# Key parts without GpSimd, weights prepared a place later: one opening of a four-layer attention kernel

## The chip, the cores and the metric

The kernel runs on one core of a Trainium2 chip. The metric is the device time of one execution in microseconds (us); the time before is the median of three runs. The engines are named as in the profile: PE is TensorE's matrix products (PEld its weight loads), DVE is VectorE, ACT is ScalarE, POOL is GpSimd, SP is SyncE, which only issues transfers here.

## What is computed

Four residual layers, A, B, A, B, over a sequence of 2048 tokens of 640 features in 32 heads of 20; both A layers share their weights, and so do both B layers. The change touches the first layer A only:

```python
phi = lambda t: jnp.where(t > 0, t + 1, jnp.exp(t)) + 1e-6
pq, pk = phi(q), phi(k)
kv = jnp.einsum("bhsd,bhse->bhde", pk, v)
z = jnp.einsum("bhsd->bhd", pk)
num = jnp.einsum("bhqd,bhde->bhqe", pq, kv)
den = jnp.einsum("bhqd,bhd->bhq", pq, z)[..., None] + 1e-6
o = num / den
# x = x + A(layernorm(x)); x = x + B(layernorm(x)); twice
```

Layer B is a block-wise softmax attention with a memory; it is not touched.

## The kernel before

**Tiles and segments.** The sequence is cut into four segments of 512 tokens, each of four tiles of 128. Every float32 operand of a product is held as two float16 parts, a high part (rounded) and a low part (what is left), and a product is three float16 products. A weight is prepared by `w_prep`: load into a staging buffer (two of them), the largest magnitude by five reductions on DVE (L239), a transpose and a broadcast on PE (L247, L253) with small steps on DVE between them (L244, L249), a power-of-two scale, then five casts on ACT for the high parts (L263) and five operations on DVE for the low parts (L264, called its splits here), and a store to DRAM. Seven weights are prepared in the opening: q, v and o of layer A, then v, q, k and o of layer B (Bv, Bq, Bk, Bo); k of layer A comes ahead of all.

**The first layer A** runs in `opening`, which weaves two streams: the main one is `g_first` for a segment, the other (`aux`) gets two steps (three in segment 0) after each of its steps. A step is a piece of a generator up to its `yield`; a step with nothing to do only lets time pass.

- `keys(i)`: for both halves of a tile a projection on PE (L394, fifteen products), exp and relu on ACT (L406, L408) and their combination e on DVE (L409). Here, in the first layer (`L["early"]`): e times a scale on POOL (L531), the high part on ACT (L532), the low part on POOL (L533), and the sum z of all keys (L541; a copy, L539, for the first tile), on DVE in segment 0 and on POOL from then on. In the second layer A the scale is taken along by ACT (L535) and DVE (L536), and POOL has no part in it.
- `queries(i)`: the same projection, then 1e-6 is added (L547, on POOL in the first layer, on DVE in the second) and the half is written to DRAM from SP's queue (L548).
- `memory()`: the products of keys and normalized input, x-hat (`xs`), ten groups of twelve (L562), added up on DVE (L567, L569).
- `merge`, at the end of segment 3: z is summed over tokens by a product with a square of ones (L610 sets it on POOL, L614 is the product), reciprocals on DVE (L616 to L620), then ten pieces `ge` (L634 to L637) and products with the value and output weights (L650, L682, L687), which give one matrix for the layer's second half.

**Beside it** `aux` holds the layer norm of the next segment (`norms`: statistics on DVE, a power on POOL in L342, x-hat on ACT in L367), its transposes on PE (`turn`: L318, high part on ACT in L322, low part on DVE in L323), its two parts (`parts`: L475 on ACT, L476 on POOL), and the weights. In segment 0: the remaining turns of this segment and weight q by turns, then the next segment's norms, then v. Segment 1: norms, o, the constants, Bv. Segment 2: norms, Bq, Bk. Segment 3: Bo, the gates, the head of the second half.

**What sets the order.** PE runs in the order of the program. The other engines' orders are laid out by a planner from priorities and estimated times; `issue_after(ins)` puts what is traced in it behind an instruction on that instruction's engine. Every engine works its own list in order, so an instruction that waits holds up all behind it. Buffers: eight PSUM banks; five buffers (`pq`) for the e of keys and queries; eleven row buffers.

Of the kernel before, what the change touches and what calls it, by code (L numbers as in the profile page):

```python
# [2 lines left out]

# [1 line left out]

# [8 lines left out]
AF = mybir.ActivationFunctionType  # L14
OP = mybir.AluOpType
AX = mybir.AxisListType
# [4 lines left out]
S, D, H, DH = 2048, 640, 32, 20  # L21
P = 128
C = D // P
# [5 lines left out]
HN = 320  # L29
# [113 lines left out]
class Kernel:  # L143
# [81 lines left out]
        return self.sb.tile([P, C, 2, D], F16, tag="wo" if o else "w", name="w_%s%s" % key,  # L225
                            bufs=2 if o else 3)

    def w_prep(self, key, stage, w, wait=0):


        nc, cp = self.nc, self.cp
        st = stage.tile([P, C, D], F32, tag="stage", name="stage", bufs=2)
        src = self.w_src(key).rearrange("(c p) n -> p c n", p=P)
        mx = cp.tile([P, C], F32, name="wmx", tag="wmx", bufs=2)
        for c in range(C):
            nc.sync.dma_start(st[:, c], src[:, c])
        yield from pause(wait)
        for c in range(C):
            nc.vector.tensor_reduce(mx[:, c:c + 1], st[:, c], axis=AX.X, op=OP.max,  # L239
                                    apply_absolute_value=True)  # L240
        yield 0.0
        yield 0.0
        m1 = cp.tile([P, 1], F32, name="wm1", tag="wm1", bufs=2)
        nc.vector.tensor_reduce(m1, mx, axis=AX.X, op=OP.max)  # L244
        yield 0.0
        pt = self.bank()
        nc.tensor.transpose(pt[:1, :P], m1, self.ident)  # L247
        m2 = cp.tile([1, 1], F32, name="wm2", tag="wm2", bufs=2)
        self.last = nc.vector.tensor_reduce(m2, pt[:1, :P], axis=AX.X, op=OP.max)  # L249
        yield 100.0  # L250
        yield from pause(wait)
        pb = self.bank()
        nc.tensor.matmul(pb[:, :1], self.ones, m2, start=True, stop=True)  # L253
        inv = cp.tile([P, 1], F32, name="inv_%s%s" % key)
        scl = cp.tile([P, 1], F32, name="scl_%s%s" % key)
        nc.vector.tensor_scalar(inv.bitcast(I32), pb[:, :1].bitcast(I32), 0x7F800000, None,
                                op0=OP.bitwise_and)
        nc.vector.tensor_scalar(inv, inv, 2.0 ** -14, 2.0 ** -114, op0=OP.mult, op1=OP.max)
        self.last = nc.vector.reciprocal(scl, inv)
        self.inv[key], self.scl[key] = inv, scl  # L260
        yield 100.0
        for c in range(C):
            nc.scalar.activation(w[:, c, 0], st[:, c], AF.Copy, scale=scl)  # L263
            self.last = nc.vector.scalar_tensor_tensor(w[:, c, 1], st[:, c], scl, w[:, c, 0],  # L264
                                                       op0=OP.mult, op1=OP.subtract)
            if c < C - 1:
                yield 0.0
        wd = self.dr.tile([P, C, 2, D], F16, name="wd_%s%s" % key)
        nc.sync.dma_start(wd, w)
        self.wd[key] = wd  # L270
        yield 0.0
# [39 lines left out]
    def turn(self, src, dst, i):  # L311

        nc = self.nc
        for c0, c1 in ((0, 3), (3, 5)):
            pt = self.bank()
            n = c1 - c0
            for c in range(c0, c1):
                nc.tensor.transpose(pt[:, (c - c0) * P:(c - c0 + 1) * P], src[:, c * P:(c + 1) * P],  # L318
                                    self.ident)
            v = pt[:, :n * P].rearrange("p (c t) -> p c t", c=n)  # L320
            hi = dst[:, c0:c1, 0, i * P:(i + 1) * P]
            nc.scalar.activation(hi, v, AF.Copy)  # L322
            nc.vector.tensor_tensor(dst[:, c0:c1, 1, i * P:(i + 1) * P], v, hi, op=OP.subtract)  # L323
            yield n * 110.0

    def load_x(self, src, s, i, name="x"):
# [187 lines left out]
    def g_first(self, s, box, w, L, behind=None):  # L514
# [7 lines left out]
        def keys(i):  # L522
            pk.append(sb.tile([P, 2, D + 1], F16, tag="row", name="pk", bufs=ROWS))
            nc.gpsimd.memset(pk[i][:, 0, HN:HN + 1], 1.0)
            nc.gpsimd.memset(pk[i][:, 1, HN:HN + 1], 0.0)
            for n in range(2):
                z, c = slice(n * HN, (n + 1) * HN), slice(n * (HN + 1), n * (HN + 1) + HN)
                e = self.phi_a(self.proj_n(xT, w("k"), i, n), self.inv["A", "k"])
                hi, lo = pk[i][:, 0, c], pk[i][:, 1, c]
                if L["early"]:  # L530
                    nc.gpsimd.tensor_tensor(e, e, self.k_scl.to_broadcast([P, HN]), op=OP.mult)  # L531
                    nc.scalar.activation(hi, e, AF.Copy)  # L532
                    nc.gpsimd.tensor_tensor(lo, e, hi, op=OP.subtract)  # L533
                else:
                    nc.scalar.activation(hi, e, AF.Copy, scale=self.k_scl)  # L535
                    nc.vector.scalar_tensor_tensor(lo, e, self.k_scl, hi, op0=OP.mult, op1=OP.subtract)  # L536
                vec = nc.gpsimd if L["early"] and s > 0 else nc.vector
                if s == 0 and i == 0:
                    vec.tensor_copy(L["z"][:, z], e)  # L539
                else:  # L540
                    vec.tensor_tensor(L["z"][:, z], L["z"][:, z], e, op=OP.add)  # L541
                yield self.COST_N

        def queries(i):
            for n in range(2):
                e = self.phi_a(self.proj_n(xT, w("q"), i, n), self.inv["A", "q"])
                (nc.gpsimd if L["early"] else nc.vector).tensor_scalar(e, e, 1e-6, None, op0=OP.add)  # L547
                nc.sync.dma_start(L["pqd"][s][i][:, n * HN:(n + 1) * HN], e)  # L548
                yield self.COST_N

        def memory():
# [41 lines left out]
    def merge(self, L, wv, wo, memory, fill):  # L593
# [13 lines left out]
        zb = sb.tile([P, MW], F32, tag="mem", name="zb", bufs=2)  # L607
        rz = self.row("rz")
        square = sb.tile([P, 512], F32, tag="er", name="square", bufs=3)[:, :P]
        nc.gpsimd.memset(square, 1.0)  # L610
        for n in range(2):
            c = slice(n * HN, (n + 1) * HN)
            p = self.bank()[:, :HN]
            nc.tensor.matmul(p, square, L["z"][:, c], start=True, stop=True)  # L614
            if L["early"]:
                nc.vector.tensor_scalar(zb[:, c], p, self.k_inv, S * 1e-6, op0=OP.mult, op1=OP.add)  # L616
            else:
                nc.vector.tensor_scalar(zb[:, c], p, S * 1e-6, None, op0=OP.add)
            nc.vector.reciprocal(rz[:, c], zb[:, c])
            nc.vector.tensor_scalar(rz[:, c], rz[:, c], self.k_inv, G_ONE, op0=OP.mult, op1=OP.mult)  # L620
            yield 4 * HN * COL
# [448 lines left out]
    def opening(self, src, stage, L, box):  # L1070
# [3 lines left out]
        def prep(key, keep=True):  # L1074
            w = self.w_tile(key) if keep else stage.tile([P, C, 2, D], F16, tag="split", name="split", bufs=1)
            if keep:
                self.w[key] = w
            yield from self.w_prep(key, stage, w, 0 if key[0] == "A" and keep else 3)

        def a(n):  # L1080
            if n not in preps:
                preps[n] = prep(("A", n), n in "kq")
            return preps[n]
# [6 lines left out]
        def late():  # L1090
            self.setup_late(stage)
            yield 0.0

        def last():
            self.scales("B")
            self.gates()
            yield 0.0
# [18 lines left out]
        m = [m]  # L1116
        with self.tc.issue_after(self.last.ins):
            m += [self.moments(x[i]) for i in range(2, NT)]
        top = self.taken

        def others():
            self.parts(first, cur[2], 0)
            for i in range(1, NT):
# [1 line left out]
                yield from self.turn(xh, cur[1], i)  # L1125
                self.parts(xh, cur[2], i)

        def later(gen):
            with self.tc.issue_after(top.ins):
                r = next(gen)  # L1130
            yield r
            yield from gen

        o = others()
        self.ones_columns()
        for s in range(NSEG):
            nxt = []
            if s == 0:
                aux = chain(turns(o, later(a("q"))), self.norms(src, 1, nxt, 6), a("v"))
            elif s == 1:  # L1140
                aux = chain(self.norms(src, 2, nxt, 6), a("o"), late(), prep(("B", "v"), False))
            elif s == 2:
                aux = chain(self.norms(src, 3, nxt, 6), prep(("B", "q"), False), prep(("B", "k"), False))
            else:
                self.scales("A")
                self.w["A", "v"] = self.fetch(("A", "v"))
                aux = chain(prep(("B", "o")), last(), self.a_head(L, 0, box))
            use = w if s < NSEG - 1 else lambda n: self.w["A", n]
            yield from weave(self.g_first(s, cur, use, L), aux, per=2 if s else 3)
            cur = nxt  # L1150
# [139 lines left out]
```

## Time and profile before

| | us |
|---|---|
| median of 3 runs (lowest, highest) | 1757.29 (1756.29, 1758.80) |
| the profiled execution | 1756.07 |
| its span, first to last instruction | 1754.4 |
| PE busy in the span | 1659.4 |
| DVE / ACT / POOL busy | 1231.1 / 991.2 / 604.6 |
| mean granted clock of PE | 0.99 |

In the profile a group's row has line, engine, operation, output and inputs, count, then busy time and mean duration in ns, then the idle time of the engine just before these instructions and what ended most of it. A timeline row has start and length in us and, in brackets, the idle time before it. A row of stretches has, for each engine, the busy time and the number of instructions in the stretch, then PE's granted clock (1.00 is full speed), the share of the DMA engines that is busy, and GB/s.

### The profile page before, as it was taken

How to read it: one execution, taken by the hardware profiler on the slowest of the kernel's cores; microseconds unless marked ns; L12 is line 12 of the kernel's file. 1: busy time of each engine (PE TensorE's matmuls, PEld its weight loads, DVE VectorE, ACT ScalarE, POOL GpSimd, SP SyncE). 2: the span in 40 equal slices, each digit the busy share in tenths (PEclk: the TensorE clock that was granted, in tenths of full speed). 3: DMA queues.
4: the chain of work that ended last, by engine and by line, in shares of the span. 5: the costliest groups of instructions: out<-in, count | busy, mean ns of one | idle time of the engine just before them, and what ended most of it. 6: DMA issues, size and time to landing. Idle time of an engine off the chain costs nothing.

```text
span 1754.4 us, 36272 instructions
## 1 busy us (share of the span) xinstructions
PE 1659.4 (95%) x13032; PEld 1033.9 (59%) x13032; DVE 1231.1 (70%) x3908; ACT 991.2 (56%) x1883; POOL 604.6 (34%) x1117
## 2 busy tenths in 40 slices
PE   6889989999999999999999999999999999999998
PEld 3656756664466456556556777666545545645555
DVE  7756667377877768767874465845878877878773
ACT  5654433336756655667676463333576576676674
POOL 4564572214313342333342210220322432332452
PEclk9989989999999999999999999999999999999999
DMA  5424435232322332334220313423222323323332
GB/s 212 170 96 173 173 121 184 96 121 66 107 70 66 104 123 77 110 125 158 67 69 31 114 38 109 157 99 132 73 90 96 107 75 108 106 77 114 133 111 91
DMA packets 113437, 190.89 MB, mean 109 GB/s; under 512 B 14172, under 2 KB 73692, under 8 KB 110696
## 3 DMA queue, kind: packets, MB, share of 16 engines
q1 hardware_dynamic: 102312, 147.93, 25.6%
q10 hardware_dynamic: 9216, 20.98, 3.1%
q0 software_dynamic: 1728, 19.66, 3.0%
q8 instruction: 103, 1.69, 0.4%
q14 instruction: 78, 0.64, 0.1%
HBM read 109.32 MB, written 78.64 MB: 107 GB/s over the span
## 4 chain that ended last, share of the span: by engine, by line
PE 64%; DVE 12%; ACT 7%; POOL 6%; issue 3%; DMA 2%; SPq 0%; ACTq 0%; POOLq 0%; DVEq 0%
PE ps L394 25%; PE ps L380 13%; PE ps L996 7%; PE ps L969 3%; PE ps L928 3%; ACT pe L973 3%; PE ps L318 3%; PE ps L562 3%; DVE ps L934 2%; PE ps L445 2%; PE ps L813 2%; PE ps L1009 1%; POOL e L547 1%; POOL e L531 1%; DVE xn L471 1%
## 5 line engine op out<-in xcount | busy, mean ns | idle before, releaser
L934 DVE CUSTOM_DVE_ANT_0 ps<-ps,maskw 128x384 f32<-128x384 f32 (+3 forms) x1024 | 472.7, 518 | 39.5 <-PE ps L928 36.8
L973 ACT ACTIVATE pe<-ps,lsc 128x512 f32<-128x512 f32 x640 | 395.8, 697 | 76.6 <-PE ps L969 71.7
L980 POOL TENSOR_SCALAR_AFFINE_SELECT pe<-pe 128x256 f32<-128x256 f32 (+1 forms) x640 | 229.7, 366 | 369.7 <-ACT pe L973 363.1
L394 PEld LDWEIGHTS <-xT 128*128 128x128 f16 x2880 | 282.7, 99 | 121.3 <-issue 10.7
L394 PEld LDWEIGHTS <-oT 128*128 128x128 f16 x1920 | 185.1, 98 | 82.1 <-issue 5.9
L996 PE MATMUL ps<-pe,v 128*32 128x512 f32 (+3 forms) x2048 | 164.4, 436 | 12.5 <-POOL pe L980 7.3
L394 PE MATMUL ps<-w_Ak,xT 128*128 128x320 f16 x960 | 144.0, 307 | 5.4 <-DVE w_Ak L264 2.2
L562 PE MATMUL ps<-pk,xs 128*128 128x321 f16 (+1 forms) x960 | 143.3, 307 | 6.1 <-POOL pk L533 3.2
L394 PE MATMUL ps<-w_Bo,oT 128*128 128x320 f16 x960 | 142.2, 301 | 1.4 <-ACT oT L322 0.7
L394 PE MATMUL ps<-wm,oT 128*128 128x320 f16 x960 | 141.7, 299 | 1.9
L380 PE MATMUL ps<-xT,w_Bq 128*128 128x512 f16 x600 | 140.3, 379 | 3.1 <-ACT r L418 1.9
L934 DVE DVE_READ_ACCUMULATOR2_ANT mg<- 128x1 f32 x1024 | 142.8, 140 | 0.0
L394 PE MATMUL ps<-w_Aq,xT 128*128 128x320 f16 x960 | 139.5, 302 | 1.6 <-DVE xT L323 1.2
L394 PE MATMUL ps<-w_Bv,xT 128*128 128x320 f16 x960 | 139.7, 299 | 1.2 <-DVE otok L1016 1.2
L380 PE MATMUL ps<-xT,w_Bk 128*128 128x512 f16 x600 | 138.3, 379 | 1.2 <-ACT pe L973 1.2
L409 DVE SCALAR_TENSOR_TENSOR e<-e,r 128x320 f32<-128x320 f32 x128 | 71.1, 559 | 84.8 <-ACT r L408 83.0
L928 PE MATMUL ps<-ks,qs 60*128 60x512 f16 (+3 forms) x1024 | 122.9, 297 | 6.7 <-ACT pe L973 3.2
L562 PEld LDWEIGHTS <-xs 128*128 128x128 f16 x960 | 95.2, 100 | 47.4 <-issue 8.9
L778 DVE SCALAR_TENSOR_TENSOR nat<-ps,nat 128x512 f16<-128x512 f32 x80 | 55.1, 689 | 83.2 <-ACT nat L777 83.0
L996 PEld LDWEIGHTS ps<-pe,v 128*32 128x32 f32 x2048 | 65.5, 109 | 74.5 <-issue 39.3
L969 PE MATMUL ps<-qs,ks 62*128 62x512 f16 (+3 forms) x1024 | 106.3, 300 | 2.3 <-ACT pe L973 1.1
L469 POOL TENSOR_TENSOR xn<-xn,xo 128x320 f32<-128x320 f32 x56 | 49.0, 876 | 145.3 <-ACT xn L468 141.1
(200 smaller groups left out, 2454.3 us busy)
## 6 DMA issues: line engine op xcount, KB each, us to landing
x<-xn ACTq DMA_DIRECT2D x48, 320.0 KB
qs<-qd SPq DMA_DIRECT2D x128, 120.0 KB
ks<-kd SPq DMA_DIRECT2D x128, 120.0 KB
xo<-x SPq DMA_DIRECT2D x48, 320.0 KB
pqd<-e SPq DMA_DIRECT2D x64, 160.0 KB
pqi<-pqd SPq DMA_DIRECT2D x32, 320.0 KB
qd<-nat SPq DMA_DIRECT2D x40, 256.0 KB
kd<-nat SPq DMA_DIRECT2D x40, 256.0 KB
```

The lines of the kernel that those rows point to most:

```text
L318: nc.tensor.transpose(pt[:, (c - c0) * P:(c - c0 + 1) * P], src[:, c * P:(c + 1) * P], self.ident)
L380: nc.tensor.matmul(p, w[:, c, a, t * P:(t + 1) * P], xT[:, c, b, :], start=k == 0, stop=k == 3 * C - 1)
L394: nc.tensor.matmul(p, xT[:, c, a, i * P:(i + 1) * P], w[:, c, b, n * HN:(n + 1) * HN], start=k == 0, stop=k == 3 * C - 1)
L409: nc.vector.scalar_tensor_tensor(e, e, 1.0, r, op0=OP.min, op1=OP.add)
L562: nc.tensor.matmul(p, xs[:, i, a, c * P:(c + 1) * P], pk[i][:, b, cols], start=k == 0, stop=k == 3 * NT - 1)
L778: nc.vector.scalar_tensor_tensor(nat[:, 1], p, QK_SHIFT, nat[:, 0], op0=OP.mult, op1=OP.subtract)
L928: nc.tensor.matmul(bs[par][:, a:a + n], qs[r, p, i * P:(i + 1) * P], ks[r, p, :n], start=True, stop=True)
L934: nc.vector.tensor_tensor_reduce(bs[par][:, a:a + n], bs[par][:, a:a + n], self.maskw[:, SEG - n:], 1.0, NEG, OP.add, OP.max, G["mg"][:, p ...
L969: nc.tensor.matmul(b[:, a:a + n], ks[r, p, j * P:(j + 1) * P], qs[r, p, j * P:], start=True, stop=True)
L973: nc.scalar.activation(e, b, AF.Exp, scale=self.lsc)
L980: nc.gpsimd.affine_select(d, d, pattern=pat, compare_op=OP.is_ge, fill=0.0, base=0, channel_multiplier=-1)
L996: nc.tensor.matmul(G["pv"][32 * h4:32 * h4 + 32, j * P:], v[j][:, h * E1:h * E1 + 32], G.pop((p, par, j)), start=j == 0, stop=j == 2, skip ...
```

## The change

In the first layer A:

1. Keys: the scale is taken along by ACT (high part) and DVE (low part), as in the second layer; POOL's two operations go. z adds up the unscaled keys, on POOL in all segments, and `merge` no longer multiplies it by the inverse scale.
2. Queries: 1e-6 is added on DVE, and the write to DRAM is issued from POOL's queue instead of SP's.
3. The square of ones in `merge` is set on DVE (in both layers A).
4. Weight q: three empty steps ahead of its maxima and three ahead of its broadcast, and the maxima are put behind the last low part of a turn that has been traced by then (they were behind the statistics of the fourth tile). The first two steps of the turns now come without steps of q between them.
5. From v on, each weight starts a place later: segment 0 has q; segment 1 v, o and the constants; segment 2 Bv and Bq; segment 3 Bk and Bo.

```diff
-    def w_prep(self, key, stage, w, wait=0):
+    def w_prep(self, key, stage, w, wait=0, behind=False):
...
-        for c in range(C):
-            nc.vector.tensor_reduce(mx[:, c:c + 1], st[:, c], axis=AX.X, op=OP.max,
-                                    apply_absolute_value=True)
+        with self.tc.issue_after(self.lower.ins) if behind else nullcontext():
+            for c in range(C):
+                nc.vector.tensor_reduce(mx[:, c:c + 1], st[:, c], axis=AX.X, op=OP.max,
+                                        apply_absolute_value=True)
...
-            nc.vector.tensor_tensor(dst[:, c0:c1, 1, i * P:(i + 1) * P], v, hi, op=OP.subtract)
+            self.lower = nc.vector.tensor_tensor(dst[:, c0:c1, 1, i * P:(i + 1) * P], v, hi, op=OP.subtract)
...
-                hi, lo = pk[i][:, 0, c], pk[i][:, 1, c]
-                if L["early"]:
-                    nc.gpsimd.tensor_tensor(e, e, self.k_scl.to_broadcast([P, HN]), op=OP.mult)
-                    nc.scalar.activation(hi, e, AF.Copy)
-                    nc.gpsimd.tensor_tensor(lo, e, hi, op=OP.subtract)
+                nc.scalar.activation(pk[i][:, 0, c], e, AF.Copy, scale=self.k_scl)
+                nc.vector.scalar_tensor_tensor(pk[i][:, 1, c], e, self.k_scl, pk[i][:, 0, c],
+                                               op0=OP.mult, op1=OP.subtract)
+                if s == 0 and i == 0:
+                    (nc.gpsimd if L["early"] else nc.vector).tensor_copy(L["z"][:, z], e)
                 else:
-                    nc.scalar.activation(hi, e, AF.Copy, scale=self.k_scl)
-                    nc.vector.scalar_tensor_tensor(lo, e, self.k_scl, hi, op0=OP.mult, op1=OP.subtract)
-                vec = nc.gpsimd if L["early"] and s > 0 else nc.vector
-                if s == 0 and i == 0:
-                    vec.tensor_copy(L["z"][:, z], e)
-                else:
-                    vec.tensor_tensor(L["z"][:, z], L["z"][:, z], e, op=OP.add)
+                    (nc.gpsimd if L["early"] else nc.vector).tensor_tensor(L["z"][:, z], L["z"][:, z], e, op=OP.add)
...
-                (nc.gpsimd if L["early"] else nc.vector).tensor_scalar(e, e, 1e-6, None, op0=OP.add)
-                nc.sync.dma_start(L["pqd"][s][i][:, n * HN:(n + 1) * HN], e)
+                nc.vector.tensor_scalar(e, e, 1e-6, None, op0=OP.add)
+                (self.q_pq if L["early"] else nc.sync).dma_start(L["pqd"][s][i][:, n * HN:(n + 1) * HN], e)
...
-        nc.gpsimd.memset(square, 1.0)
+        nc.vector.memset(square, 1.0)
...
-            if L["early"]:
-                nc.vector.tensor_scalar(zb[:, c], p, self.k_inv, S * 1e-6, op0=OP.mult, op1=OP.add)
-            else:
-                nc.vector.tensor_scalar(zb[:, c], p, S * 1e-6, None, op0=OP.add)
+            nc.vector.tensor_scalar(zb[:, c], p, S * 1e-6, None, op0=OP.add)
...
-            yield from self.w_prep(key, stage, w, 0 if key[0] == "A" and keep else 3)
+            yield from self.w_prep(key, stage, w, 0 if key == ("A", "k") else 3, key == ("A", "q"))
...
-                aux = chain(turns(o, later(a("q"))), self.norms(src, 1, nxt, 6), a("v"))
+                aux = chain(islice(o, 2), turns(o, a("q")), self.norms(src, 1, nxt, 6))
             elif s == 1:
-                aux = chain(self.norms(src, 2, nxt, 6), a("o"), late(), prep(("B", "v"), False))
+                aux = chain(self.norms(src, 2, nxt, 6), a("v"), a("o"), late())
             elif s == 2:
-                aux = chain(self.norms(src, 3, nxt, 6), prep(("B", "q"), False), prep(("B", "k"), False))
+                aux = chain(self.norms(src, 3, nxt, 6), prep(("B", "v"), False), prep(("B", "q"), False))
             else:
                 self.scales("A")
                 self.w["A", "v"] = self.fetch(("A", "v"))
-                aux = chain(prep(("B", "o")), last(), self.a_head(L, 0, box))
+                aux = chain(prep(("B", "k"), False), prep(("B", "o")), last(), self.a_head(L, 0, box))
```

More of the change, by code (lines that the diff above doesn't have):

```diff
@@ L1 @@
-from contextlib import ExitStack
-from itertools import chain
+from contextlib import ExitStack, nullcontext
+from itertools import chain, islice
 import numpy as np
@@ L1118, in opening @@
             m += [self.moments(x[i]) for i in range(2, NT)]
-        top = self.taken
         def others():
@@ L1126, in others @@
                 self.parts(xh, cur[2], i)
[L1128 to L1132, printed above, removed]
         o = others()
```

## The prediction

> **What bounds the kernel now.** I read the page first: busy shares, then the 40 slices.
>
> ```profile
> PE 1659.4 (95%) x13032; PEld 1033.9 (59%) x13032; DVE 1231.1 (70%) x3908; ACT 991.2 (56%) x1883; POOL 604.6 (34%) x1117
> ...
> PE   6889989999999999999999999999999999999998
> ```
>
> TensorE (PE) is busy 95% of the span and nearly full from the eighth slice on. What an edit of other engines' work can give back lies in the first seven slices, the opening. I cut it at the points where the projections, the memory products and the merge begin, and asked for busy time by stretch: segment 0, 1, 2, segment 3 up to the product with the summed keys, the rest of the merge, and all that follows.
>
> ```profile
> core 0: us, PE busy (x) PEld busy (x) DVE busy (x) ACT busy (x) POOL busy (x), PEclk, DMA share, GB/s
> 20.00:88.90 68.90, 59.35 (x389) 41.49 (x389) 54.23 (x136) 44.77 (x83) 39.30 (x57) 0.93 0.51 182
> 88.90:152.50 63.60, 56.54 (x382) 39.37 (x380) 33.91 (x72) 30.53 (x63) 41.61 (x50) 0.92 0.32 110
> 152.50:208.10 55.60, 53.64 (x394) 38.66 (x393) 35.87 (x70) 27.55 (x59) 29.76 (x41) 1.00 0.42 149
> 208.10:250.20 42.10, 34.14 (x240) 23.34 (x238) 24.93 (x44) 22.43 (x46) 29.13 (x33) 0.94 0.49 186
> 250.20:278.00 27.80, 26.34 (x221) 19.20 (x222) 25.65 (x56) 7.08 (x16) 10.78 (x12) 0.90 0.20 65
> 278.00:1754.40 1476.40, 1423.20 (x11396) 868.53 (x11393) 1042.11 (x3501) 849.91 (x1604) 448.48 (x900) 1.00 0.30 101
> ```
>
> Length less PE busy gives PE's idle time: 9.6, 7.1, 2.0, 8.0 and 1.5 us. The granted clock below 1.00 is a second loss: (1 - clock) times length is 4.8, 5.1, 0, 2.5 and 2.8 us. So 28 us idle and 15 us of slow clock, 43 us, is all that the opening can return. The gaps, from PE's own timeline (the last bracket is the idle time before the row and what ended it):
>
> ```profile
> 28.36 0.72 PE L394 MATMUL ps<-w_Ak,xT 128*128 128x320 f16 x4 [1.76 <-DVE xT L323]
> 31.11 0.37 PE L247 MATMUL ps<-ident,wm 128*1 128x128 f32 x1 [1.82 <-DVE wm L244]
> 47.62 0.90 PE L318 MATMUL ps<-ident,xh 128*128 128x128 f32 x3 [3.70 <-ACT xh L367]
> 51.80 0.30 PE L562 MATMUL ps<-pk,xs 128*128 128x321 f16 x1 [0.87 <-ACT pk L532]
> 53.50 0.43 PE L562 MATMUL ps<-pk,xs 128*128 128x321 f16 x2 [1.39 <-POOL pk L533]
> ...
> 102.90 0.44 PE L318 MATMUL ps<-ident,xh 128*128 128x128 f32 x2 [0.77 <-ACT r L408]
> 105.73 0.90 PE L318 MATMUL ps<-ident,xh 128*128 128x128 f32 x3 [2.39 <-ACT r L408]
> 126.69 0.55 PE L253 MATMUL ps<-wm,ones 1*128 1x1 f32 x2 [3.67 <-DVE wm L249]
> ...
> 242.83 0.30 PE L562 MATMUL ps<-pk,xs 128*128 128x321 f16 x1 [2.08 <-ACT pk L532]
> 244.65 3.13 PE L562 MATMUL ps<-pk,xs 128*128 128x321 f16 x14 [1.52 <-POOL pk L533]
> 250.20 2.50 PE L614 MATMUL ps<-z,square 128*128 128x320 f32 x4 [2.42 <-POOL square L610]
> ```
>
> Behind most of them stands GpSimd (POOL): ScalarE (ACT) waits in its queue for the scaled keys, and so its next relu, which frees a PSUM bank, is late too. Groups by line, 20 to 278 us:
>
> ```profile
> L532 ACT ACTIVATE pk<-e 128x320 f16<-128x320 f32 x32 | 15.1, 471 | 53.9 <-POOL e L531 53.5
> ...
> L547 POOL TENSOR_SCALAR e<-e 128x320 f32<-128x320 f32 x31 | 34.7, 1120 | 17.2 <-DVE e L409 16.3
> L533 POOL TENSOR_TENSOR pk<-e,pk 128x320 f16<-128x320 f32 x32 | 27.4, 855 | 2.6 <-ACT pk L532 2.5
> L531 POOL TENSOR_TENSOR e<-e,k_scl 128x320 f32<-128x320 f32 x32 | 24.9, 779 | 34.8 <-DVE e L409 29.1 <-DVE scl_Aq L259 2.4 <-issue 2.1
> L541 POOL TENSOR_TENSOR z<-z,e 128x320 f32<-128x320 f32 x24 | 22.8, 949 | 1.7
> ```
>
> The first row is the case for the change: 53.5 us of ScalarE's idle time ends with a GpSimd multiplication.
>
> **The change, part by part.** The second layer A already runs the new form; its rows, and the group of the adds that move, price it:
>
> ```profile
> L535 ACT ACTIVATE pk<-e,k_scl x32: 562/566/637, 819.8 to 1088.6; 128x320 f16<-128x320 f32 x32
> L536 DVE SCALAR_TENSOR_TENSOR pk<-e,k_scl,pk x32: 542/552/1505, 820.4 to 1089.2; 128x320 f16<-128x320 f32 x32
> L547 DVE TENSOR_SCALAR e<-e x32: 308/326/871, 827.9 to 1123.0; 128x320 f32<-128x320 f32 x32
> ...
> L541 DVE TENSOR_TENSOR z<-z,e 128x320 f32<-128x320 f32 x6 | 4.5, 756 | 0.9 <-POOL e L531 0.9
> ```
>
> *Engines.* GpSimd loses 34.7 + 27.4 + 24.9 = 87 us and gains eight z operations at 0.949, 7.6 us. VectorE gains 32 low parts at 0.552 and 32 additions of 1e-6 at 0.326, 17.7 + 10.4 = 28.1 us, and loses segment 0's z, 4.5 us and two copies: about +23 us. ScalarE gains 32 x (0.566 - 0.471) = 3 us and loses most of the 53.5 us wait. The memset of the square goes from GpSimd to VectorE, under 0.2 us. A key's chain is one GpSimd link shorter.
>
> *What stretches.* VectorE is slowed while GpSimd works beside it:
>
> ```profile
> L409 DVE SCALAR_TENSOR_TENSOR e<-e,r 128x320 f32<-128x320 f32 x63 | 38.0, 610 | 39.2 <-ACT r L408 37.6 <-POOL z L541 0.8 <-issue 0.3
> L239 DVE TENSOR_REDUCE wmx<-stage 128x1 f32<-128x640 f32 x35 | 27.5, 808 | 15.7 <-DMA stage<-in_B_wq 6.2 <-DMA stage<-in_B_wo 6.1 <-DMA stage<-in_B_wv 1.7
> L264 DVE SCALAR_TENSOR_TENSOR split<-stage,scl_Ao,split 128x640 f16<-128x640 f32 x5 | 6.6, 1354 | 0.1
> L264 DVE SCALAR_TENSOR_TENSOR split<-stage,scl_Bk,split 128x640 f16<-128x640 f32 x5 | 4.2, 876 | 0.0
> ```
>
> The same split of a weight costs 1354 ns a piece in the busiest stretch of GpSimd and 876 elsewhere, a factor of 1.55. With GpSimd's work more than halved I take the free price for the added low parts; at the factor they cost 27.4 us in place of 17.7. The Trainium skill, "GPSIMD Engine Reference", section 8 "Key points", names this: GpSimd shares its SBUF interfaces with VectorE, and they collide when a VectorE instruction has two SBUF inputs. The splits agree. By that rule each added low part, which reads two tiles, collides with the z adds and the xs parts that stay on GpSimd, so up to 10 us of VectorE time would come back, and the sum would be nearer the third rival's.
>
> *Weights.* One weight costs VectorE five maxima and five splits, 5 x 0.808 + 5 x 0.876 = 8.4 us. The list (q, v, o, Bv, Bq, Bk, Bo) keeps its order, but from v on each starts a place later: segment 0 loses one, segments 1 and 2 trade one for one, segment 3 has two (Bk, Bo) where it had Bo. Their loads stay on SP and move with them; VectorE's waits for loads (6.2 and 6.1 us in the L239 row above) are counted unchanged.
>
> *The DMA queue of the queries.* 32 transfers go from SP to GpSimd's queue. Before, SP spent 0.32 us on each; GpSimd's transfers in the trace are ten times larger:
>
> ```profile
> L548 SPq DMA_DIRECT2D pqd<-e x64: 319/320/707, 79.8 to 1123.4; - x64
> L275 POOL DMA_DIRECT2D w_Av<-wd_Av x2: 617/700/782, 208.6 to 1062.9; - x2
> w_Ak<-wd_Ak POOLq DMA_DIRECT2D x1, 1600.0 KB, 9.1
> ...
> 72.58 16.46 PE L394 MATMUL ps<-w_Aq,xT 128*128 128x320 f16 x120
> ```
>
> I take 0.70 us of issue, 22 us on GpSimd, covered by the 87 that it loses. Each issue waits for VectorE's addition, and queued behind it are z adds, the powers of the norms and the xs parts. The price can sit in the five buffers of e: segment 0 makes eight queries in 16.46 us, 2.06 each, so a buffer may be held 10.3 us. Exp and relu at about 0.57 each, 0.61, 0.33, 0.70 and the 9.1 of a ten times larger transfer make 11.9: (11.9/5 - 2.06) x 8 = 2.6 us at worst. For a tenth of the size I take nothing, and keep 0 to +2.6.
>
> *Segment 0* (14.4 us to be had). The maxima behind the turns free the 1.76 us gap, but the turns now come without maxima between them and up to two yields sooner, so a transpose can wait for its xh instead: I count neither a gain nor a loss there. The next segment's norms come six yields later, so the 3.70 gap is replaced by a wait for the last keys, some 1.5: -2.2. The pk gaps (0.87 and 1.39) close: -2.3. A third of the slow clock (4.8) goes with them: -1.6. Together **-6**; 0 if the wait for xh takes it all, -13 if all but 1.4 closes.
>
> *Segment 1* (12.2). The 2.39 gap and its 0.77 forerunner come from ScalarE stuck behind GpSimd: -3. The 3.67 gap, a weight's second maximum queued behind e on VectorE, shrinks to about 1: -2.7. Their clock stretches:
>
> ```profile
> 105.55:108.97 3.42, 3.24 (x13) 1.97 (x14) 2.81 (x6) 2.83 (x8) 2.82 (x4) 0.50 0.13 48
> 1062.50:1094.30 31.80, 31.80 (x236) 22.92 (x235) 18.11 (x38) 17.45 (x36) 1.35 (x3) 1.00 0.37 133
> 1094.30:1122.00 27.70, 24.47 (x223) 18.11 (x222) 27.18 (x57) 6.95 (x16) 9.73 (x11) 1.00 0.18 58
> ```
>
> The first row is the 3.42 us at half clock right behind the 2.39 gap, 1.7 us lost; I count two of three such stretches: -3.4. Together **-9** (-4 to -12). The Trainium skill, "TensorE: Matmul & The Clock Gate", "HAM oscillation", says that idle gaps above about 3.4 us are to be avoided. Here 2.39 us was enough, so the measurement decides, and the gaps that I leave keep their price; by the page they would cost no clock, and the sum would be some 5 us lower.
>
> *Segment 2*: 0 (-2 to +3): the 2.0 us idle are all there is.
>
> *Segment 3.* The second row is its twin in the second layer: 31.80 us against 42.10, PE full, no weights. So 10.3 us could go. But VectorE would hold 24.93 + 8.4 (Bk) + 8 x 0.552 + 6 x 0.326 = 39.7 us of work in it, or 37.3 if Bo's splits lose their stretch (5 x 0.876 x 0.55 at most): over 5 more than PE. VectorE becomes late, and with its own waits I take 40: **-2** (-10 to +8).
>
> *Merge*: the third row has no GpSimd keys either, and is as long, 27.7 against 27.8, for VectorE is full in both. Nothing to gain; the slow clock there was hidden. If Bo's five splits (4.4 us) slip into it they are paid: **+1** (0 to +4.4).
>
> Sum: -6 - 9 + 0 - 2 + 1 = -16. The profiled execution took 1756.07 (span 1754.4 and 1.7 around it), 1.2 below the median, 1757.29, so 1741 beside the median. After 278 us PE's order is unchanged and I count nothing.
>
> **The rivals.**
> 1. *All closes, as in the second layer*: -13 - 11 - 2 - 10 = -36, **1721**. For it: 31.80 us with PE full. Against: no weights are prepared there.
> 2. *VectorE takes over half*: segments 0 and 1 give 4 each, segment 3 nothing: -8, **1749**.
> 3. *Given back*: segments 0 and 1 give half, -7.5, and segment 3 with the merge costs as much: **1757**, no change.
> 4. *Slower: VectorE's queue in segment 3.* Its 37.3 us are worked off at the share that it was busy there before, 24.93 of 42.10 or 59%: 63 us, +21; Bo's splits in the merge +4.4; segments 0 and 1 give half, -7.5: **1775**; with a share of 65 to 75% some 1762 to 1769. It decides once VectorE is busy for less than 37.3/42.1 = 89% of the segment. For it: its waits on ScalarE's relu (37.6 us in the opening) remain. Against: part of these are GpSimd's, handed on.
>
> **How the numbers follow.** Forecast 1741 (own range 1729 to 1748): 0.46; first rival 0.10; second 0.10; third 0.08; fourth 0.26. About 0.2%, 3.5 us, can be told from no change in this kernel. Faster 0.66, same 0.08, slower 0.26. The range, 1722 to 1772, leaves out about 0.07 below and 0.11 above; most chance lies on two sides, so the likeliest's own range stands above.
>
> **What would show it.** Right: ScalarE's wait for L531 is gone, segment 1 near 55 us, the 53.50, 105.73, 242.83 and 250.20 gaps closed, VectorE above 85% in segment 3. Wrong: PE waiting for VectorE's low parts or maxima (L239, L244, L249) at segment 3's memory products or in the merge, z late because GpSimd waits in a DMA issue, or slow clock left in segments 0 and 1.

## The result, and the profile after

The changed kernel takes 1751.64 us (median of 12 runs, 1748.41 to 1754.61), the kernel before 1759.16 us beside it (12 runs, 1753.83 to 1761.54). The ratio is 0.9959, with a 95% interval of 0.9948 to 0.9969: 7.2 us faster, less than half of the 16 that were forecast. The profiled execution took 1753.38 us, its span 1751.6.

The page's first part and PE's slices of the kernel after; the busy shares hardly move, and the opening is still where PE is not full:

```profile
PE 1658.7 (95%) x13032; PEld 1034.7 (59%) x13032; DVE 1252.5 (72%) x3966; ACT 994.8 (57%) x1883; POOL 541.2 (31%) x1059
...
PE   5999988999999999999999999999999999999998
```

Cut at PE's first product of each stage (keys of the next segment, the product with the summed keys, the first product with `wo`'s matrix, the first products with Bv and Bq), the stages last, in us (segments 1 and 2 meet at 153.39 here, where the prediction's rows were cut at 152.50):

| stage | before | after | change | forecast |
|---|---|---|---|---|
| segment 0 (from 20) | 68.9 | 65.8 | -3.1 | -6 |
| segment 1 | 64.5 | 52.2 | -12.3 | -9 |
| segment 2 | 54.8 | 53.4 | -1.3 | 0 |
| segment 3, up to the product with z | 42.1 | 38.9 | -3.2 | -2 |
| merge | 27.8 | 33.9 | +6.2 | +1 |
| products with `wo` | 10.7 | 10.7 | 0 | 0 |
| head of the second half, up to Bv | 21.2 | 28.8 | +7.6 | 0 |

The sum up to the first product with Bq (327.14 before, 321.06 after) is -6.1. The same cut as stretches of the kernel after (columns as in the prediction; the sixth row is `wo` and head, the last the rest):

```profile
20.00:85.80 65.80, 57.59 (x386) 40.59 (x386) 55.05 (x143) 41.70 (x78) 33.49 (x52) 0.95 0.44 159
85.80:138.00 52.20, 52.20 (x388) 38.06 (x386) 37.27 (x82) 34.93 (x68) 21.02 (x35) 1.00 0.31 106
138.00:191.40 53.40, 52.38 (x388) 38.07 (x386) 42.61 (x85) 28.10 (x59) 12.09 (x20) 1.00 0.46 167
191.40:230.30 38.90, 34.61 (x242) 24.18 (x240) 27.44 (x60) 20.85 (x43) 10.73 (x15) 0.96 0.59 217
230.30:264.20 33.90, 26.05 (x222) 19.40 (x221) 31.62 (x66) 9.92 (x21) 10.83 (x13) 0.85 0.31 110
264.20:303.70 39.50, 34.09 (x233) 20.51 (x231) 20.63 (x55) 10.60 (x26) 6.03 (x8) 0.91 0.58 217
303.70:1751.60 1447.90, 1395.59 (x11168) 850.52 (x11165) 1023.54 (x3447) 839.77 (x1579) 441.66 (x891) 1.00 0.30 97
```

Segment 1 is full: 52.20 busy of 52.20, at full clock. From segment 3 on PE has idle time of 4.3, 7.9 and 5.4 us and a lower clock, and the last of these stretches was 31.75 us long in the kernel before, with PE busy for 31.21:

```profile
277.95:309.70 31.75, 31.21 (x231) 19.12 (x229) 19.98 (x55) 10.47 (x26) 6.60 (x8) 1.00 0.71 258
```

PE's gaps in the kernel after, from its timeline (the bracket is the idle time before the row and what ended it):

```profile
24.00 0.90 PE L319 MATMUL ps<-ident,xh 128*128 128x128 f32 x3 [2.11 <-ACT xh L368]
38.87 0.37 PE L248 MATMUL ps<-ident,wm 128*1 128x128 f32 x1 [3.64 <-DVE mv L340]
50.20 0.30 PE L557 MATMUL ps<-pk,xs 128*128 128x321 f16 x1 [0.55 <-ACT pk L530]
52.27 2.08 PE L557 MATMUL ps<-pk,xs 128*128 128x321 f16 x14 [1.78 <-DVE pk L531]
...
208.21 0.38 PE L254 MATMUL ps<-wm,ones 1*128 1x1 f32 x2 [4.29 <-DVE wm L250]
251.78 0.27 PE L642 MATMUL ps<-xT,w_Av 128*128 128x140 f16 x1 [5.08 <-ACT xT L628]
...
289.03 0.55 PE L319 MATMUL ps<-ident,pqi 128*128 128x128 f32 x3 [3.61 <-POOL pqi L705]
```

The gaps of segment 1 and those in front of z are gone. Three new ones stand at 208, 252 and 289 us, one in each of the stretches that lost. Followed back in time through the timelines of VectorE, SP and GpSimd, they come from one weight, Bo, that is ready late:

```profile
193.65 2.85 SPq L236 DMA_DIRECT2D stage<-in_B_wo  x5
...
205.78 0.82 DVE L240 TENSOR_REDUCE wmx<-stage 128x1 f32<-128x640 f32 x1 [6.29 <-DMA stage<-in_B_wo]
...
230.31 1.24 PE L609 MATMUL ps<-z,square 128*128 128x320 f32 x4
...
233.62 1.67 DVE L265 SCALAR_TENSOR_TENSOR w_Bo<-stage,scl_Bo,w_Bo 128x640 f16<-128x640 f32 x2
...
235.21 0.88 DVE L610 TENSOR_SCALAR zb<-ps 128x320 f32<-128x320 f32 x2
...
235.32 0.33 SPq L270 DMA_DIRECT2D wd_Bo<-w_Bo  x1
235.83 2.64 SPq L698 DMA_DIRECT2D pqi<-pqd  x3
...
242.59 4.54 POOL L699 TENSOR_TENSOR pqi<-pqi,zb 128x640 f32<-128x640 f32 x3 [11.23 <-DMA pqi<-pqd]
...
249.94 2.77 DVE L626 SCALAR_TENSOR_TENSOR ge<-v,eps,rz 128x320 f32<-128x320 f32 x2
...
273.03 0.91 DVE L760 MEMSET one<- 2x1024 f16 x1
...
273.97 3.73 SPq L763 DMA_DIRECT2D ks<-one  x6
277.87 0.34 SPq L698 DMA_DIRECT2D pqi<-pqd  x1
...
283.91 1.53 POOL L699 TENSOR_TENSOR pqi<-pqi,zb 128x640 f32<-128x640 f32 x1 [8.12 <-DMA pqi<-pqd]
```

*Segment 3.* There are two staging buffers, so Bo's load can start only when Bq's splits are done. VectorE stands 6.29 us in front of Bo's first maximum, and behind that in its list stand e and the small reduction for Bk (L250) that PE waits for at 208.21.

*Merge.* Bo's splits stand ahead of zb, which comes 4.9 us after its product (230.31). The store of Bo waits on SP for the last split, and behind the store stand the reads of the queries (`pqi`, for the second half). GpSimd gets them at 242.59; VectorE's reductions of them are placed ahead of the first `ge`, which PE needs.

*Head.* By the program, the constant `one` lies in memory that the staging buffers had. In the kernel before its memset came right behind Bo's splits:

```profile
234.87 0.91 DVE L768 MEMSET one<- 2x1024 f16 x1 [0.27 <-DVE w_Bo L264]
```

Here the planner puts it at 273.03. (In e2 below, where Bo's splits also end behind the product with z, the memset is late too; in e1 and e9, where they end ahead of it, it follows them within 1 us. Why the planner moves it that far no run shows.) The six transfers from it wait on SP for 35.7 us, and the fourth read of the queries stands behind them: 277.87, where the others were issued at 235.83.

### The profile page after: what moved, and what is told of

Same layout as the page of the kernel before. It is cut to its first block, busy times and chain, and to the rows that moved or that the text cites. A ratio compares the mean times of both kernels' runs of the same rounds, so it can differ in the third digit from the quotient of the medians.

```text
span 1751.6 us, 36286 instructions
## 1 busy us (share of the span) xinstructions
PE 1658.7 (95%) x13032; PEld 1034.7 (59%) x13032; DVE 1252.5 (72%) x3966; ACT 994.8 (57%) x1883; POOL 541.2 (31%) x1059
## 4 chain that ended last, share of the span: by engine, by line
PE 71%; DVE 12%; ACT 7%; DMA 4%; POOL 3%; issue 2%; SPq 1%; ACTq 0%; POOLq 0%; DVEq 0%
PE ps L395 30%; PE ps L381 13%; PE ps L988 7%; PE ps L557 4%; PE ps L961 4%; PE ps L920 3%; PE ps L319 3%; ACT pe L965 3%; PE ps L446 2%; DVE ps L926 2%; PE ps L805 2%; PE ps L1001 1%; DMA pqi<-pqd 1%; DVE split L265 1%; DMA stage<-in_B_wo 1%
## 5 line engine op out<-in xcount | busy, mean ns | idle before, releaser
L557 PE MATMUL ps<-pk,xs 128*128 128x321 f16 (+1 forms) x960 | 137.4, 300 | 2.3 <-DVE pk L531 1.8
L410 DVE SCALAR_TENSOR_TENSOR e<-e,r 128x320 f32<-128x320 f32 x128 | 64.7, 505 | 56.5 <-ACT r L409 55.6
L769 ACT ACTIVATE nat<-ps 128x512 f16<-128x512 f32 x80 | 48.3, 604 | 88.3 <-PE ps L381 72.0
```

The source lines that it names most:

```text
L410: nc.vector.scalar_tensor_tensor(e, e, 1.0, r, op0=OP.min, op1=OP.add)
L557: nc.tensor.matmul(p, xs[:, i, a, c * P:(c + 1) * P], pk[i][:, b, cols], start=k == 0, stop=k == 3 * NT - 1)
```

## The experiments

Three theories. **First**: the late weights cost the time, through Bo. **Second** (the prediction's fourth rival): VectorE's added work in segment 3 does. **Third**: the queries' transfers on GpSimd's queue do. Each ratio is to the kernel before on the same chip, with its 95% interval.

**e1: the weights' places as before**, all else as after.

```diff
-                aux = chain(islice(o, 2), turns(o, a("q")), self.norms(src, 1, nxt, 6))
+                aux = chain(islice(o, 2), turns(o, a("q")), self.norms(src, 1, nxt, 6), a("v"))
...
-                aux = chain(self.norms(src, 2, nxt, 6), a("v"), a("o"), late())
+                aux = chain(self.norms(src, 2, nxt, 6), a("o"), late(), prep(("B", "v"), False))
...
-                aux = chain(self.norms(src, 3, nxt, 6), prep(("B", "v"), False), prep(("B", "q"), False))
+                aux = chain(self.norms(src, 3, nxt, 6), prep(("B", "q"), False), prep(("B", "k"), False))
...
-                aux = chain(prep(("B", "k"), False), prep(("B", "o")), last(), self.a_head(L, 0, box))
+                aux = chain(prep(("B", "o")), last(), self.a_head(L, 0, box))
```

> The changed kernel with the weights in their old places (v in segment 0, Bk in segment 2, only Bo in segment 3); all else as changed. Theory 1, the weights' shift gives back what the keys gain (Bo's load wait in segment 3, Bo's splits ahead of zb in the merge, the fourth read of the queries late on SP): the merge falls from 33.9 to about 27.8 us, the head of the second half from 39.5 to about 31.8, segment 3 to 36 to 40, segment 0 may lose 2 to 4; 12 to 18 us below the changed kernel, some 20 to 25 below before. Theory 2, VectorE has too much with the low parts and additions wherever the weights lie: merge and segment 3 stay long, within 4 us of the changed kernel. Theory 3, the queries' writes land late from GpSimd's queue: the waits of GpSimd for pqi (11.2 and 8.1 us) stay, at most 4 us gained.

Measured: 1735.78 us, 0.9864 (0.9848 to 0.9879), that is 0.95% or 16.7 us below the change's 0.9959. Its segment 3, merge, and `wo` with head, as stretches:

```profile
196.60:228.90 32.30, 32.30 (x238) 23.20 (x237) 25.25 (x53) 20.21 (x42) 11.27 (x16) 1.00 0.60 219
228.90:256.80 27.90, 24.49 (x223) 18.13 (x222) 27.44 (x57) 6.95 (x16) 10.37 (x12) 1.00 0.28 95
256.80:288.60 31.80, 31.27 (x232) 19.16 (x230) 20.45 (x56) 10.70 (x27) 6.06 (x8) 1.00 0.70 245
```

PE is full in segment 3, 32.30 of 32.30, beside the 31.80 of the second layer's twin. VectorE works 25.25 us in it where it worked 27.44 in 38.90. So most of the new form's gain was there and was given back. SP's and VectorE's timelines of e1 show Bo out of the way before z (228.90): store, memset, transfers and all four reads in a row.

```profile
217.90 0.33 SPq L270 DMA_DIRECT2D wd_Bo<-w_Bo  x1
...
218.42 0.91 DVE L760 MEMSET one<- 2x1024 f16 x1
...
219.36 5.13 SPq L763 DMA_DIRECT2D ks<-one  x6
224.65 19.00 SPq L698 DMA_DIRECT2D pqi<-pqd  x4
...
229.64 1.03 DVE L610 TENSOR_SCALAR zb<-ps 128x320 f32<-128x320 f32 x2
```

**e2: the late weights alone**, on the kernel before (the lists of the other three segments as in the change).

```diff
-                aux = chain(turns(o, later(a("q"))), self.norms(src, 1, nxt, 6), a("v"))
+                aux = chain(turns(o, later(a("q"))), self.norms(src, 1, nxt, 6))
...
-                aux = chain(prep(("B", "o")), last(), self.a_head(L, 0, box))
+                aux = chain(prep(("B", "k"), False), prep(("B", "o")), last(), self.a_head(L, 0, box))
```

> The kernel before with the weights' shift alone. Theory 1: the merge grows by 4 to 7 us and the head of the second half by 5 to 8, segment 3 by 2 to 6, segment 0 gains 0 to 4; 8 to 18 us slower than before. Theory 2: the shift alone costs under 4 us, for GpSimd still has the keys. Theory 3: no difference, as the writes are on SP.

Measured: 1764.55 us, 1.0026 (1.0017 to 1.0035), 4.6 us slower, less than the 8 to 18 of the first theory. Segment 3 is 2.8 us longer, the merge 4.2 and the head 6.7, as expected; what the theory left out is that segment 1 is 8.2 us shorter. PE's timeline has the gaps of the change at the same two places (L253 and L318 are L254 and L319 after), without the new keys and with the queries on SP:

```profile
218.35 0.58 PE L253 MATMUL ps<-wm,ones 1*128 1x1 f32 x2 [5.03 <-DVE wm L249]
...
302.23 0.90 PE L318 MATMUL ps<-ident,pqi 128*128 128x128 f32 x3 [3.81 <-POOL pqi L713]
```

**e3: the new key parts alone**, on the kernel before; z stays as it was (VectorE in segment 0).

```diff
-                if L["early"]:
-                    nc.gpsimd.tensor_tensor(e, e, self.k_scl.to_broadcast([P, HN]), op=OP.mult)
-                    nc.scalar.activation(hi, e, AF.Copy)
-                    nc.gpsimd.tensor_tensor(lo, e, hi, op=OP.subtract)
...
-                    nc.scalar.activation(hi, e, AF.Copy, scale=self.k_scl)
-                    nc.vector.scalar_tensor_tensor(lo, e, self.k_scl, hi, op0=OP.mult, op1=OP.subtract)
+                nc.scalar.activation(hi, e, AF.Copy, scale=self.k_scl)
+                nc.vector.scalar_tensor_tensor(lo, e, self.k_scl, hi, op0=OP.mult, op1=OP.subtract)
...
-            if L["early"]:
-                nc.vector.tensor_scalar(zb[:, c], p, self.k_inv, S * 1e-6, op0=OP.mult, op1=OP.add)
-            else:
-                nc.vector.tensor_scalar(zb[:, c], p, S * 1e-6, None, op0=OP.add)
+            nc.vector.tensor_scalar(zb[:, c], p, S * 1e-6, None, op0=OP.add)
```

> The kernel before with the key parts alone on ScalarE and VectorE (z of the unscaled keys, where it was: VectorE in segment 0, GpSimd after); queries, queue, square, q and all weights as before. Theory 1: the key parts are what gains. Segment 1 falls from 64.5 to 53 to 57 us, segment 3 up to the product with z from 42 to 32 to 36, merge and head as before: 15 to 24 us below before, within 6 of the kernel with only the weights put back. Rival: the additions of 1e-6, 1.1 us on GpSimd, hold the chain as well, and then at most 12 us are gained.

Measured: 1739.35 us, 0.9886 (0.987 to 0.9902), 20 us faster. Segment 1 is 59.0 long (53 to 57 were expected) and segment 3 32.3. Most of one edit of the five has nearly three times the gain of all together. The late weights shorten segment 1 by 8.2 us when they are alone (e2), but by only 2.3 on top of the other edits (54.5 in e1, 52.2 after): little idle time is left there, while their cost further on stays.

**e4: the six transfers from `one` issued by ScalarE**, all else as after.

```diff
-                nc.sync.dma_start(k[a:a + 2], one[:2])
+                nc.scalar.dma_start(k[a:a + 2], one[:2])
```

> The changed kernel, with the six small transfers of the constant rows (ks from one), which wait for a late memset on VectorE, issued from ScalarE's queue in place of SP's. If the fourth read of the queries is late since it stands behind them in SP's order (part of theory 1): it is issued 5 to 11 us earlier, the 3.6 us gap at the transposes of pqi and the slow clock behind it go, the head of the second half falls from 39.5 to 32 to 34 us, the whole by 4 to 8 us; the merge stays at 33.9. Theory 3: the read is no earlier than the queries' writes allow, no change over 2 us. ScalarE could itself be held up by the wait for the memset (up to +5).

Measured: 1744.5 us, 0.9907 (0.9893 to 0.992), 9 us below the change. The head falls from 28.8 to 20.4, the gap at its transposes is gone; segment 3 (38.5) and merge (34.2) stay. The memset is as late as in the kernel after; the fourth read no longer stands behind it:

```profile
237.01 9.21 SPq L698 DMA_DIRECT2D pqi<-pqd  x4
...
274.50 0.91 DVE L760 MEMSET one<- 2x1024 f16 x1
```

The Trainium skill, "Trainium Kernel Development and Optimization", "Key Constraints", says that issuing from several engines only saves the issue time. Here the six issues take 3.73 us on SP, and PE's stage became 8.4 us shorter: what was saved was the wait of the read that stood behind them.

**e5: weight q as before**, all else as after (no empty steps, its maxima behind the statistics of the fourth tile, the turns by turns with it).

```diff
-            yield from self.w_prep(key, stage, w, 0 if key == ("A", "k") else 3, key == ("A", "q"))
+            yield from self.w_prep(key, stage, w, 0 if key[0] == "A" and keep else 3)
...
-                aux = chain(islice(o, 2), turns(o, a("q")), self.norms(src, 1, nxt, 6))
+                aux = chain(turns(o, later(a("q"))), self.norms(src, 1, nxt, 6))
```

> The changed kernel with weight q's maxima placed as before (behind the statistics of the fourth tile, no empty steps, turns and q in turn from the first step). Theory A, the new place costs what it frees: the 3.6 us gap at q's first transpose and its 6.8 us of half clock go, the old gaps of 1.8 and 1.8 with one half-clock stretch return: 0 to 3 us less than the changed kernel. Theory B, the new place was a gain in segment 0: 3 to 6 us slower than the changed kernel.

Measured: 1750.76 us, 0.995 (0.9937 to 0.9964), not to be told from the change. Segment 0 is 65.3 (after 65.8): the new place of q's maxima gives nothing. The 3.64 gap at 38.87 goes, and gaps of 1.92, 2.72 and 3.76 come.

**e6: the queries' writes on SP again**, all else as after.

```diff
-                (self.q_pq if L["early"] else nc.sync).dma_start(L["pqd"][s][i][:, n * HN:(n + 1) * HN], e)
+                nc.sync.dma_start(L["pqd"][s][i][:, n * HN:(n + 1) * HN], e)
```

> The changed kernel with the queries' writes on SP's queue again. Theory 1: they hardly matter; on SP they wait for e in the list ahead of weight loads, so 0 to 5 us slower than the changed kernel, and the reads of pqi are as late (GpSimd's waits of 11.2 and 8.1 us for them stay). Theory 3, the writes land late from GpSimd's queue: these waits shrink by 3 us or more and the kernel gains 3 to 8.

Measured: 1754.3 us, 0.9968 (0.9955 to 0.998). The intervals overlap: GpSimd's queue costs nothing that can be measured. GpSimd's waits for `pqi` do not shrink (14.80 and 8.23 us, after 11.23 and 8.12), and the third theory falls.

**e7: e1 and e5 together**: new keys, queries, z and square; weights and q as before.

> The changed kernel with the weights put back and weight q's maxima as before as well: what is left of the change is the key parts, the queries' addition and queue, and the square. If q's place hardly matters, within 3 us of the kernel with the weights alone put back (1736), and 0 to 4 us below the kernel with the key parts alone (1739). If q's place was a gain with the weights in their old places, 3 to 6 us above 1736.

Measured: 1733.03 us, 0.9849 (0.9834 to 0.9863): 26.6 us faster than before, 19 faster than the change, and the best of all. Against e1 the intervals overlap. Against e3 they don't (0.9863 and 0.987 are the near ends): the queries, z and square give some 6.5 us more.

**e8: Bo's store issued by ScalarE**, all else as after, so that the reads of the queries don't stand behind it.

```diff
-        nc.sync.dma_start(wd, w)
+        (nc.scalar if key == ("B", "o") else nc.sync).dma_start(wd, w)
```

> The changed kernel with Bo's store to DRAM, behind which the first three reads of the queries stand on SP in the merge, issued from ScalarE's queue. Theory 1 in its finer form: of the merge's 6 us about 3 are Bo's splits ahead of zb (they stay) and 3 are these reads, issued only at 235.8 us; they are now issued 4 us or more earlier, GpSimd starts on them at zb and the first ge comes 2 to 4 us sooner: merge 30 to 32 us in place of 33.9, the whole 2 to 5 below the changed kernel. Rival: the whole of it is Bo's splits, and the merge stays within 1 us of 33.9.

Measured: 1746.8 us, 0.9925 (0.9912 to 0.9939), 6 us below the change. The merge falls from 33.9 to 30.4. SP issues the reads 14 us sooner; GpSimd now waits for zb, and `ge` comes 3.4 us sooner:

```profile
221.40 2.90 SPq L698 DMA_DIRECT2D pqi<-pqd  x3
...
236.72 4.53 POOL L699 TENSOR_TENSOR pqi<-pqi,zb 128x640 f32<-128x640 f32 x3 [4.82 <-DVE zb L610]
...
246.50 2.29 DVE L626 SCALAR_TENSOR_TENSOR ge<-v,eps,rz 128x320 f32<-128x320 f32 x2
```

**e9: Bk alone back in segment 2** (Bv, Bq and Bk there; Bo alone in segment 3), to see whether two weights in segment 3 are what hurts.

```diff
-                aux = chain(self.norms(src, 3, nxt, 6), prep(("B", "v"), False), prep(("B", "q"), False))
+                aux = chain(self.norms(src, 3, nxt, 6), prep(("B", "v"), False), prep(("B", "q"), False), prep(("B", "k"), False))
...
-                aux = chain(prep(("B", "k"), False), prep(("B", "o")), last(), self.a_head(L, 0, box))
+                aux = chain(prep(("B", "o")), last(), self.a_head(L, 0, box))
```

> The changed kernel with Bk alone back in segment 2 (which then has Bv, Bq and Bk; v stays in segment 1). Theory 1: what hurts is two weights in segment 3, not the later start of v. Segment 3, merge and head as with all weights put back (about 32, 28 and 32 with the head), segment 1 as in the changed kernel (52): 14 to 20 us below the changed kernel. Theory 2: VectorE is the bound, three weights in segment 2 make it 5 us or more longer there, and the kernel gains under 8.

Measured: 1750.08 us, 0.9945 (0.9931 to 0.9958), not to be told from the change. Merge (28.4) and head (21.1) are cured, but segment 2 is 59.1 long and segment 3 43.6, and PE's gaps are larger:

```profile
195.47 0.37 PE L248 MATMUL ps<-ident,wm 128*1 128x128 f32 x1 [4.18 <-DVE wm L245]
...
213.99 0.37 PE L248 MATMUL ps<-ident,wm 128*1 128x128 f32 x1 [6.66 <-DVE wm L245]
```

So the finer form of the first theory, that only the number of weights in segment 3 counts, falls: it holds for merge and head alone. The second theory's numbers for this run came out: segment 2 is 5.6 us longer, and the kernel gains under 3. In the 8 us up to the first of these gaps VectorE works without a break (187.39 to 195.42: Bq's splits, Bk's maxima, the additions of the memory products), so there its list is what PE waits for. With two staging buffers each load waits for the splits of the weight two places ahead; a chain that begins a place late stays late, and packed into fewer steps it makes PE wait for a weight's maxima instead. A third staging buffer was not tried.

**e10: e4 and e8 together.**

> The changed kernel with both blockers taken off SP's queue: Bo's store and the six ks transfers go from ScalarE's queue. If the late reads of the queries on SP are what these two edits each cured by themselves, they add up: merge about 30.5 us, head of the second half 21 in place of 28.8, 10 to 13 us below the changed kernel; what is left against the kernel with the weights put back (about 16 below the changed kernel) is Bo's splits ahead of zb and the load wait in segment 3. If ScalarE's queue is then held by the store's wait, less than 8.

Measured: 1740.39 us, 0.9889 (0.9873 to 0.9906), 12 us below the change. Merge is 30.5 and head 20.4; segment 3 keeps its wait for Bo's load (38.7). Alone the two edits gave 9 and 6. The two queue orders are worth 12 of the 16.7 us that e1 gives, in the same places. What is left to e7 at the first product with Bq (310.79 less 302.06) is 8.7 us, of which 6.4 in segment 3 and 3.3 in the merge, where Bo's splits still stand ahead of zb; that these two are the load and the splits is read from the rows, not tried by itself.

## Why the prediction was half right

**The bound, and the way to it**: right. The opening was where time could be had, and GpSimd behind ScalarE's queue was its cause. e3, which does only that, gains 20 us. Groups of the kernel after, 20 to 278 us:

```profile
L410 DVE SCALAR_TENSOR_TENSOR e<-e,r 128x320 f32<-128x320 f32 x64 | 32.0, 501 | 11.2 <-ACT r L409 10.4 <-ACT xT L323 0.5
...
L531 DVE SCALAR_TENSOR_TENSOR pk<-e,k_scl,pk 128x320 f16<-128x320 f32 x32 | 25.1, 783 | 8.3 <-ACT pk L530 8.3
L543 POOL DMA_DIRECT2D pqd<-e x32 | 18.0, 564 | 47.6 <-DVE e L542 31.5 <-DVE wm L250 9.1 <-DVE split L265 2.4
L530 ACT ACTIVATE pk<-e,k_scl 128x320 f16<-128x320 f32 x32 | 18.0, 563 | 32.1 <-DVE e L410 32.0
...
L542 DVE TENSOR_SCALAR e<-e 128x320 f32<-128x320 f32 x32 | 13.2, 412 | 0.6
```

ScalarE's 53.5 us behind GpSimd are gone; it now waits 32.0 us for e itself, one link earlier. VectorE's wait for relu, which the prediction called GpSimd's handed on, fell from 37.6 to 10.4 us.

**Segment 0**, -6 for -3.1. The 3.70 gap went, but "neither a gain nor a loss" for q's new place was wrong: q's five maxima stand between e and key parts (33.51 to 38.25 on VectorE), PE waits 3.64 us to transpose what the next row makes of them, and 2.11 for the x-hat of an earlier turn.

```profile
38.57 0.15 DVE L245 TENSOR_REDUCE wm<-wmx 128x1 f32<-128x5 f32 x1
```

(The gap's bracket names the operation behind that, L340, which ended last on VectorE.) The pk gaps (0.87 and 1.39) did not close; they are 0.55 and 1.78. With the slow clock down from 10.2 to 6.8 us of half clock, that is 1.3 us of idle time and 1.7 of clock.

**Segment 1**, -9 for -12.3: the mechanism right, the size short; all of it closed. **Segment 2**, 0 for -1.3, within its bounds.

**Segment 3**, -2 for -3.2, the right size by the wrong reason. The term took VectorE to be over full, above 85%; it was busy 27.44 of 38.90, 71%, and it waited for a load. Its work was not the 37.3 to 39.7 us that the term added up: Bk's first three maxima lie ahead of the segment and Bo's splits behind z. Without the late weights the segment takes 32.3, nearly the twin's 31.80, with VectorE at 78%. The fourth rival, VectorE's queue at 59 to 75%, falls with it.

**The added low parts** were taken at the free price, 0.552 (17.7 us). They cost 0.783 (25.1 us), near the 27.4 at the stretch, and the additions 0.412 for 0.326. Here the Trainium skill ("GPSIMD Engine Reference", "Key points") was the better guide: low parts read two tiles and met GpSimd's z. Laid beside GpSimd's timeline, the 25 low parts that overlap one of its operations took 0.72 us (median), the 7 that don't 0.54. The prediction's "876 elsewhere" was read too widely as well: in the kernel before, Bq's splits in segment 2 took 1.197 us each, with GpSimd busy 7.50 of the 8.60 us around them. In return e, freed of GpSimd's multiplications (36 of the 54 that stand singly in the timeline overlapped a GpSimd operation before, 6 of 64 do after), fell from 0.610 to 0.501, 7.0 us over 64, which takes back most of the 10.2 us that low parts and additions cost beyond the forecast.

**The queries' queue**, 0: right (e6). An issue took 0.564 us, not 0.70.

**The merge and what follows are the step that failed.** The prediction said that loads "are counted unchanged", that only Bo's splits could slip into the merge, +1 (0 to +4.4), and that after 278 us "PE's order is unchanged and I count nothing". The merge lost 6.2 us and the head 7.6. PE's order was unchanged, but SP's list hung on Bo's last split and on the memset of `one`. The prediction followed the loads and the splits that move, and left out what waits for a moved weight's last instruction: a store with reads behind it (e8), a constant in the staging buffers' memory with transfers and a read behind it (e4). By the forecast for these stages (+1) the stages' sum would have been -19; the 13 us above it are the miss.

**The third rival**, given back, had the right shape and the wrong place: not half of segments 0 and 1 lost in segment 3, but 15.4 us won in them and 13.8 lost behind z. **The second rival**'s -8 is the number nearest to the result, by luck: it had 4 us from each of segments 0 and 1 and nothing lost later. **The first**, all closes as in the second layer, was set against weights being prepared; with their places as before, e7 comes to it in segment 3 (32.3) and the merge (27.2), and gains 26.6 of its 36 us. By these runs the change would have been a clear gain without its fifth part.

The profiled spans differ by 2.8 us where the stages differ by 6.1: the rest of the kernel after is 3.3 us longer in that one execution, with two stretches of half clock in it, 601.07 to 604.49 and 1386.14 to 1389.55. The medians, 7.5 us apart, stand above single executions.

## What to carry to other kernels

A step that is moved later moves everything that waits for its last instruction: follow its store, the buffer that it frees and what lies in that memory afterwards into every queue, and see what stands behind them there. Two edits that close the same gap gain it once, but each brings its own cost, so run each alone before keeping both. Where an issuing engine's list holds a transfer that waits, a second issuing engine is worth more than its issue time says.

## What the runs showed of the hardware

Half clock came behind gaps of very different lengths. In the kernel after it followed 5.08, 4.29, 3.64 and 3.61 us, but the 2.11 gap was followed by none until 37.88, whereas the prediction's 2.39 had cost 3.42 us of half clock at once. At the place of the 2.11, a gap of 2.74 us in e1, e4 and e8 came with 6.8 us of half clock, one of 2.10 in e6, e9 and e10 with none; yet in e3 the 1.64 us before 102.41 were followed by 3.4. The length of the gap alone does not decide. In the openings of all twelve kernels the stretches are multiples of 3.4 us, from 3.4 to 10.2, as in the windows of the last two in the opening:

```profile
249.50:259.74 10.24, 5.19 (x34) 3.91 (x34) 10.05 (x23) 4.26 (x9) 3.35 (x6) 0.50 0.00 0
290.46:297.29 6.83, 6.10 (x24) 3.48 (x25) 4.03 (x11) 2.52 (x6) 0.55 (x1) 0.50 0.28 97
```

And a write of 160 KB from GpSimd's queue landed in 2.1 us (median of 32), with issues of 0.564: a quarter of the landing, 9.1, of the ten times larger transfer that the prediction had for a bound.
